# Talking-heads attention and a leaky MLP in one program: a ring of eight regrouped tiles, and a reordered end of the attention

## The chip, the cores and the metric

The kernel runs on one core of one Trainium2 chip. The metric is the device time of one execution in microseconds; lower is better. Engines are named as in the profile: PE is TensorE's matmul, PEld its weight load, DVE VectorE, ACT ScalarE, POOL GpSimd and SP SyncE, which here only issues DMAs.

## The reference, cut to what matters

Four batches, 12 heads, 448 positions, 64 channels; then an MLP on 1792 tokens of 768 channels with 2048 hidden ones. All is float32. The heads are mixed by `w_pre` ahead of the softmax and by `w_post` behind it.

```python
def _attn_ref(q, k, v, w_pre, w_post):
    scores = 1.0 / np.sqrt(q.shape[-1]) * np.matmul(q, k.transpose(0, 1, 3, 2))
    scores = np.einsum('bhij,hg->bgij', scores, w_pre)
    attn = np.exp(scores - np.max(scores, axis=-1, keepdims=True))
    attn = attn / (np.sum(attn, axis=-1, keepdims=True) + 1e-09)
    attn = np.einsum('bhij,hg->bgij', attn, w_post)
    return np.matmul(attn, v)

def reference(q, k, v, w_pre, w_post, moe_w_in, moe_w_out):
    a = _attn_ref(q, k, v, w_pre, w_post)          # B, H, S, D
    x = a.transpose(0, 2, 1, 3).reshape(B * S, H * D)
    h = x @ moe_w_in
    return np.maximum(0.01 * h, h) @ moe_w_out
```

## The kernel before, in words

**Attention.** The queries are cut into 16 chunks `n`, four to a batch, of 120, 120, 120 and 88 rows. A chunk is worked in three periods `s`, so there are 48 periods. Ten query rows with their 12 heads make a group of 120 partitions, two groups make a quad; a full chunk has six quads, the last chunk of a batch five.

- `scores(n, a)` (L184) multiplies queries and keys of a head pair into PSUM; `move` (L197) copies them on ScalarE into the score tile `s_t[n]`. This is done two chunks ahead, two pairs in a period. There are two score tiles.
- `regroup(n, a, z)` (L207) brings groups out of the score tile into `r` tiles by DMA, so that the heads of a row lie on partitions: even groups are issued by SyncE, odd ones by GpSimd. There are 12 `r` tiles (L205), used in turn. `transfers` (L610) calls it one chunk ahead, at the slots 1, 2, 4, 6, 8 and 10 of a chunk's twelve, two groups at a time (L27).
- `first(n, s, u)` (L216) mixes the heads of a quad by `w_pre` into a PSUM tile `psm` (two buffers), `maxima` (L230) takes the row maxima on VectorE, `power` (L235) the exponentials and their sums on ScalarE into `et`.
- `weights(n, s)` (L245) makes `kp` on VectorE: `w_post` times the reciprocal of the sums. `mix(n, s, part)` (L259) multiplies `et` by `kp` in two halves into `psa`; the first half is copied by ScalarE, the second by VectorE (L308). `values(n, s)` (L310) multiplies by V, one chunk behind; `keep_x` (L331) copies on VectorE and `store_x` (L338) writes to memory. `psa`, `psx` and the scores `pss` share two PSUM buffers of two banks.

Beside this the MLP's weights, which arrive as 64-bit words, are made float32 in pieces (`Narrow`, L83): a load `craw` (SyncE), two activations `z` and `w` (ScalarE, L102 and L103), three operations on VectorE, two on GpSimd, and a store (SyncE). A period spreads one piece, and two in seven of the 48; the main loop loads pieces until four less the period's count are loaded (L722).

**The order** of nearly all of the attention is written out: `pin` keeps each engine's instructions, and each queue's DMAs, in program order. So a DMA that waits holds all that stands behind it on its queue. Where `pin` is not used (the MLP's splits, sums and output), a planner orders the work by its own model of the times.

**The end of the attention** (`end_period`, L630) takes the last two chunks' six periods, without scores. It also loads the attention's output back (`load_x`, L358, four tiles to a call and two DMAs to a tile) and prepares it for the MLP (`prep_x`, L375: sums on GpSimd, a cast on ScalarE, a rest on VectorE, three or four parts in a period).

**The MLP.** Each float32 operand is split into a rounded part and a rest (`split`, L399), and each product is three matmuls. Batches `p` go in pairs; `hidden(p, j, stage)` (L472) forms two column blocks for two batches from seven products in place of eight (sums of x and w are formed ahead), in two PSUM banks `h1` and `h2`. `keep` (L454) applies the leaky maximum, `summed` (L465) adds a copied product to PSUM first. `project(u)` (L512) multiplies a hidden block by `w_out` into six PSUM banks; at a batch's end each bank is copied to an `o` tile (five of them, L803) and written out. In the pair's last units `load_x` and `prep_x` get the next pair's x (L809 to L815).

## Time and profile before

| | us |
|---|---|
| median of 3 runs | 901.79 (901.67, 901.79, 906.54) |
| profiled execution, its own time | 910.94 |
| its span, first to last instruction | 909.0 |
| PE busy | 822.5 (90%) |
| DVE busy | 590.3 (65%) |
| ACT busy | 487.4 (54%) |
| POOL busy | 170.6 (19%) |
| mean granted TensorE clock | 0.964 |

All times in rows are microseconds from the span's start unless marked ns. An engine's busy time leaves out its waits. TensorE's matmuls overlap and their ends are modelled, so a busy PE is not a PE at its peak. A granted clock of 1.00 is 2.4 GHz, of 0.50 it is 1.2 GHz; a mean between them tells the share of time at each.

### The profile page before, as it was taken

Reading aid. Unit: us, or ns where it says so; the run is one execution under the profiler, and the core shown is the slowest. Engines: PE = TensorE matmul, PEld = TensorE weight load, DVE = VectorE, ACT = ScalarE, POOL = GpSimd, SP = SyncE. Lnnn points to the kernel's source line nnn. Section 1 sums busy time; section 2 is a strip of 40 time slices with the busy share of each in tenths; the row PEclk is TensorE's granted clock in tenths of the full one; section 3 lists DMA queues with packets and bytes.
Section 4 is the critical chain, followed back from the end, with each engine's and each line's share of the span. In section 5 each row is a group of like instructions: output and inputs, shape, how many; then the busy total and the mean of one; then the engine's idle time right before and its main releaser. Section 6 shows DMA issues by size and latency. Waiting matters only on the chain.

```text
span 909.0 us, 25915 instructions
## 1 busy us (share of the span) xinstructions
PE 822.5 (90%) x10904; PEld 659.4 (73%) x10904; DVE 590.3 (65%) x1063; ACT 487.4 (54%) x952; POOL 170.6 (19%) x224
## 2 busy tenths in 40 slices
PE   7789988898889898967789999998999999999998
PEld 3356655565556555646679999997999999999897
DVE  5368666586656676766788778876756656653443
ACT  3577767687675776736254454535544333432432
POOL 4144353343443344342200000000000000000000
PEclk9699999899898999989899999999999999999999
DMA  6996969786986769473245434426634222221533
GB/s 171 266 268 197 246 214 268 194 256 211 260 241 193 235 199 271 147 203 102 82 161 172 146 122 140 148 88 197 176 104 156 80 70 74 84 70 39 161 106 112
DMA packets 90768, 150.60 MB, mean 166 GB/s; under 512 B 33001, under 2 KB 63245, under 8 KB 90653
## 3 DMA queue, kind: packets, MB, share of 16 engines
q1 hardware_dynamic: 80808, 125.50, 46.8%
q0 software_dynamic: 7296, 19.40, 8.1%
q10 hardware_dynamic: 2548, 4.06, 1.4%
q8 instruction: 86, 1.41, 0.7%
q14 instruction: 30, 0.24, 0.1%
HBM read 85.73 MB, written 23.59 MB: 120 GB/s over the span
## 4 chain that ended last, share of the span: by engine, by line
PE 72%; issue 9%; ACT 5%; DVE 5%; DMA 4%; SPq 3%; POOL 1%; POOLq 0%; DVEq 0%; ACTq 0%
PE pso L148 25%; PE psh L148 22%; PE psx L148 8%; PE pss L148 6%; PE psm L148 6%; PE psa L148 5%; ACT st L198 3%; DMA craw<-in_w_moe 2%; ACT et L241 1%; SPq L212 1%; DVE stat L231 1%; DMA qt<-in_q 1%; DMA r<-st 1%; DVE top L111 1%; SPq L370 1%
## 5 line engine op out<-in xcount | busy, mean ns | idle before, releaser
L148 PEld LDWEIGHTS psa<-kp,et 64*64 64x64 f32 x5888 | 112.4, 140 | 84.6 <-issue 52.9
L148 PE MATMUL psa<-kp,et 64*64 64x60 f32 (+1 forms) x5888 | 115.0, 222 | 39.3 <-issue 23.1
L148 PE MATMUL pso<-gh,wl 128*128 128x448 f32 x384 | 141.5, 369 | 5.1 <-DVE wl L403 3.3
L148 PE MATMUL pso<-gl,wh 128*128 128x448 f32 x384 | 140.9, 367 | 0.0
L148 PE MATMUL pso<-gh,wh 128*128 128x448 f32 x384 | 140.9, 367 | 0.0
L241 ACT ACTIVATE et<-psm,stat 128x448 f32<-128x448 f32 x184 | 116.0, 639 | 18.2 <-DVE stat L231 13.4
L198 ACT ACTIVATE st<-pss 120x896 f32<-120x896 f32 (+1 forms) x84 | 77.1, 918 | 90.3 <-PE pss L148 90.1
L231 DVE TENSOR_REDUCE stat<-psm 128x2 f32<-128x896 f32 x92 | 99.7, 1086 | 38.6 <-PE psm L148 38.5
L402 ACT CAST wh<-wo 128x768 fp32r<-128x768 f32 x64 | 53.3, 835 | 127.1 <-PE pso L148 121.5
L403 DVE TENSOR_TENSOR wl<-wo,wh 128x768 fp32r<-128x768 f32 x64 | 61.1, 956 | 86.2 <-ACT wh L402 86.2
L148 PE MATMUL pss<-kt,qt 64*56 64x448 f32 (+2 forms) x768 | 103.1, 578 | 8.5 <-DMA qt<-in_q 2.9
L148 PE MATMUL psm<-r,kpre 64*64 64x448 f32 x736 | 101.0, 595 | 8.0 <-ACT et L241 3.1
L119 POOL TENSOR_TENSOR w<-w,z 128x384 f32<-128x384 f32 x48 | 47.9, 998 | 205.1 <-ACT et L241 143.5
L148 PEld LDWEIGHTS pso<-gh,wl 128*128 128x128 f32 x384 | 72.5, 189 | 13.0 <-DVE wl L403 4.9
L148 PE MATMUL psx<-at,vt 128*64 128x120 f32 (+1 forms) x1152 | 69.9, 272 | 12.5 <-issue 4.8
L148 PEld LDWEIGHTS pso<-gh,wh 128*128 128x128 f32 x384 | 72.6, 189 | 5.8
L148 PEld LDWEIGHTS pso<-gl,wh 128*128 128x128 f32 x384 | 72.6, 189 | 5.7
L148 PEld LDWEIGHTS psx<-at,vt 128*64 128x64 f32 x1152 | 58.8, 140 | 18.4 <-ACT st L198 8.6
L333 DVE COPY xo<-psx 128x240 f32<-128x240 f32 (+1 forms) x48 | 27.4, 570 | 68.8 <-PE psx L148 68.8
L148 PEld LDWEIGHTS pss<-kt,qt 64*64 64x64 f32 (+2 forms) x768 | 29.3, 134 | 40.2 <-PE pss L148 18.1
L212 POOL DMA_DIRECT2D r<-st x90 | 53.4, 595 | 22.2 <-PE psm L148 18.9
L148 PEld LDWEIGHTS psm<-r,kpre 64*64 64x64 f32 x736 | 27.8, 141 | 39.2 <-issue 26.5
(101 smaller groups left out, 1466.0 us busy)
## 6 DMA issues: line engine op xcount, KB each, us to landing
craw<-in_w_moe SPq DMA_DIRECT2D x64, 384.0 KB
wo<-w_dram SPq DMA_DIRECT2D x64, 384.0 KB
r<-st SPq DMA_DIRECT2D x92, 210.0 KB
r<-st POOLq DMA_DIRECT2D x90, 210.0 KB, 6.4
wi<-w_dram SPq DMA_DIRECT2D x34, 384.0 KB
w_dram<-w SPq DMA_DIRECT2D x64, 192.0 KB
kt<-in_k SPq DMA_DIRECT2D x42, 112.0 KB
vt<-in_v SPq DMA_DIRECT2D x12, 384.0 KB
```

What stands on the lines that cost most here:

```text
L111: pin(nc.vector.scalar_tensor_tensor(top, z.bitcast(U32), 0x80000000, top, op0=ALU.bitwise_and, op1=ALU.bitwise_or))
L119: pin(self.joiner.tensor_mul(w, w, self.exp))
L148: pin(nc.tensor.matmul(*args, **kw))
L198: pin(nc.scalar.activation(to, ps, AF.Copy, scale=scale))
L212: pin((queues or (nc.sync, nc.gpsimd))[g % 2].dma_start(t[LOW:LOW + RH], s_t[n][g:m:m // ROWS]))
L231: pin(nc.vector.tensor_reduce(e_t[n, s][1][:, 0, 2 * u:2 * u + 2], ps[:, :, :S], axis=AX.X, op=ALU.max, negate=True))
L241: pin(nc.scalar.activation(e, ps[:, y, :S], AF.Exp, bias=st[:, 0, g:g + 1], accum_out=st[:, 1, g:g + 1]))
L333: pin(nc.vector.tensor_copy(xo_t[n][:, RUN * s:RUN * (s + 1), :m].rearrange("p a (x g) -> p a g x", x=ROWS), ps[:, :RUN, :m].rearrange("p ...
L370: pin(nc.sync.dma_start(t[:, full:], rest[:, c + HC * h]))
L402: hold(nc.scalar.copy(hi, raw))
L403: hold(nc.vector.tensor_sub(lo, raw, hi.bitcast(F32)))
```

## The change

**The ring.** Eight `r` tiles instead of twelve. `refill(count)` places the next `count` groups in order of the whole program, each by one DMA, in the tile that the group eight places earlier has left. It is called right behind the `first` calls that read those tiles: at the start 4 + 4, then 4; in the main loop behind the maxima of the period's first quad, and behind the second score pair for its second quad; in the last periods likewise. The calls from `transfers` go.

**The end.** `weights` of the next period is made at the end of this one's first mix half, instead of at the start of its own. The second quad's exponentials come behind the copy of the first mix half. `load_x` stays ahead, `prep_x` moves behind the second mix half. The very last `values` has a PSUM buffer of its own. `prep_wi(0, 2)` is pinned.

**The MLP.** `keep` is one Prelu on ScalarE. Product 7 is copied out of PSUM and product 5 is added to it there, where before product 5 was copied and product 7 stayed. The next pair's x is loaded tile by tile: eight tiles from the fourth block on, the last four in the units behind. Six `o` tiles instead of five.

```diff
@@ -24,7 +24,7 @@
 QUAD = 2 * ROWS
-REGROUP = (1, 2, 4, 6, 8, 10)
+RING = 8
@@ -201,14 +201,15 @@
-    turn = [0]
-    r_all = [p_r.tile([P, S], F32, tag=f"r{i}", name=f"r{i}") for i in range(SLOTS)]
-
-    def regroup(n, a, z, *queues):
-        m = width(n)
-        for g in range(a, min(z, m // ROWS)):
-            r_t[n, g] = t = r_all[turn[0] % SLOTS]
-            turn[0] += 1
+    r_all = [p_r.tile([P, S], F32, tag=f"r{i}", name=f"r{i}") for i in range(RING)]
+    groups = [(n, g) for n in range(NCK) for g in range(width(n) // ROWS)]
+    placed = iter(range(len(groups)))
+
+    def refill(count, *queues):
+        for _, i in zip(range(count), placed):
+            n, g = groups[i]
+            m = width(n)
+            r_t[n, g] = t = r_all[i % RING]
             pin((queues or (nc.sync, nc.gpsimd))[g % 2].dma_start(
@@ -307,12 +308,12 @@
-    def values(n, s):
+    def values(n, s, pool=ps_x):
         b, m = chunks[n][0], width(n)
...
             xo_t[n] = p_x.tile([P, NPAIR, CHUNK], F32, tag="xo", name="xo")
-        ps = ps_x.tile([P, 2, 512], F32, tag="x", name="psx")[:, 0].rearrange("p (a i) -> p a i", a=4)
+        ps = pool.tile([P, 2, 512], F32, tag="x", name="psx")[:, 0].rearrange("p (a i) -> p a i", a=4)
         w = v_t[b, s]
@@ -355,19 +356,19 @@
-    def load_x(p, c):
-        for e in range(2):
-            for h in range(2):
...
+    def load_x(p, c, tiles=range(4)):
+        for i in tiles:
+            e, h = divmod(i, 2)
...
@@ -451,15 +452,10 @@
-    def keep(p, j, m, e, c, out_of_psum=False):
+    def keep(p, j, m, e, c):
         g = pl["g"].tile([P, S], F32, tag=f"g{e}", name=f"g{e}", bufs=NF if e else 4)
         g_t[2 * p + e, 2 * j + m] = g
-        if out_of_psum:
-            t = pl["g"].tile([P, S], F32, tag="p1", name="t", bufs=1)
-            nc.scalar.activation(t, c, AF.Copy, scale=0.01)
-            nc.vector.tensor_max(g, t, c)
-        else:
-            nc.vector.scalar_tensor_tensor(g, c, 0.01, c, op0=ALU.mult, op1=ALU.max)
+        nc.scalar.activation(g, c, AF.Prelu, alpha=0.01)
@@ -486,14 +482,14 @@
             product(7, hid[2], True)
+            p7 = copy_of(hid[2], "p1")
             product(5, hid[1], False)
-            u4 = copy_of(hid[1], "p1")
-            summed(p, j, 1, 1, u4, hid[2])
+            summed(p, j, 1, 1, p7, hid[1])
         if stage == 2:
...
             product(3, hid[1], False)
-            keep(p, j, 0, 1, hid[1][:, :S], True)
+            keep(p, j, 0, 1, hid[1][:, :S])
@@ -569,12 +565,13 @@
         move_half(*scores(0, a, ((ps_x, "x"), (ps_m, "m"))[a % 2]))
-    regroup(0, 0, NJ, nc.sync, nc.scalar)
-    regroup(0, NJ, SLOTS)
+    refill(NJ, nc.sync, nc.scalar)
+    refill(RING - NJ)
     for a in range(NPAIR):
...
     dues = [first(0, 0, u) for u in range(2)]
+    refill(2 * len(dues))
     for due in dues:
@@ -600,19 +597,19 @@
-    def x_work(n, t):
+    def x_loads(n, t):
         for i in x_plan.get(t + SLOTS * (n - NCK + 2), ()):
...
                 load_x(0, -1 - i)
-            else:
+
+    def x_preps(n, t):
+        for i in x_plan.get(t + SLOTS * (n - NCK + 2), ()):
+            if i >= 0:
                 prep_x(0, *divmod(i, X_PARTS), nc.gpsimd, pin)
...
     def transfers(n, s, c):
-        b, last = chunks[n][0], n == NCK - 1
+        b = chunks[n][0]
         t = NJ * s + c
-        if not last and t in REGROUP:
-            g = 2 * REGROUP.index(t)
-            regroup(n + 1, g, g + 2)
         if t == HALF + 1 and n + 3 < NCK:
@@ -651,25 +648,36 @@
             pl.update(ws=pool("ws", 1), ps_h=pool("ps_h", 1, space=PSUM))
+            pl["ps_v"] = pools(psum, "left")("ps_v", 1, space=PSUM)
         early, late = ((2, 0), (2, 1), (2, 1), (1, 0), (0, 0), (0, 0))[at]
...
             pending = None
-        weights(n, s)
+        if at == 0:
+            weights(n, s)
         dues = [first(*left_quads.pop(0)) for _ in range(early)]
...
             maxima(*due)
+        refill(2 * early)
         for c in range(NJ):
             transfers(n, s, c)
-            x_work(n, NJ * s + c)
-        for due in dues:
+            x_loads(n, NJ * s + c)
+        for due in dues[:1]:
             power(*due)
         keep_at(mix(n, s, 0))
-        assemble()
+        for due in dues[1:]:
+            power(*due)
+        while spreading:
+            assemble()
+        if at < 5:
+            weights(*((n, s + 1) if s < 2 else (n + 1, 0)))
         keep_x(*values(n - 1, s))
         keep_at(mix(n, s, 1))
+        for c in range(NJ):
+            x_preps(n, NJ * s + c)
         for _ in range(late):
             due = first(*left_quads.pop(0))
+            refill(2)
             maxima(*due)
@@ -698,6 +706,7 @@
                 maxima(*due)
+            refill(2 * len(dues))
             transfers(n, s, 0)
@@ -716,6 +725,7 @@
                 move(*scores(to, pair + 1))
+            refill(2 * len(dues[1:]))
             if dues:
@@ -738,7 +748,7 @@
     for s in range(3):
-        keep_x(*values(NCK - 1, s))
+        keep_x(*values(NCK - 1, s, pl["ps_v"] if s == 2 else ps_x))
         for k in ((3,), (4,), (5, 6))[s]:
@@ -767,7 +777,7 @@
     load_wo(1)
-    prep_wi(0, 2)
+    prep_wi(0, 2, pin)
     load_wi(1)
@@ -795,12 +805,15 @@
                     unit += 1
+                ahead = 2 * j + stage - 6
+                if p == 0 and 0 <= ahead < 8:
+                    load_x(1, ahead // 4, (ahead % 4,))
                 narrow_late()
...
             extra.close()
-            pl["o"] = pools(mlp, "left")("o", NC - 1)
+            pl["o"] = pools(mlp, "left")("o", NC)
         while unit < (2 * p + 2) * NF - (2 if 2 * p + 2 < B else 0):
@@ -809,10 +822,10 @@
                 c, k = divmod(at, 4)
-                if k == 0:
-                    load_x(p + 1, c)
-                for k in range(2 * k, min(2 * k + 2, X_PARTS)):
-                    prep_x(p + 1, c, k)
+                for i in range(2 * k, min(2 * k + 2, X_PARTS)):
+                    prep_x(p + 1, c, i)
+                if c == 1:
+                    load_x(p + 1, 2, (k,))
```

## Rows read from the trace of the kernel before

**Rows 1.** Windows: length, busy PE, PEld, DVE, ACT, POOL (count), clock, DMA share, GB/s.

```profile
40.00:382.50 342.50, 300.25 (x7359) 201.57 (x7351) 229.17 (x462) 247.61 (x531) 137.35 (x172) 0.96 0.81 230
382.50:440.60 58.10, 40.74 (x1047) 30.93 (x1047) 40.56 (x73) 28.40 (x68) 21.54 (x21) 0.91 0.45 125
397.00:412.00 15.00, 9.13 (x197) 5.75 (x189) 9.19 (x13) 7.24 (x20) 5.95 (x6) 0.77 0.72 214
440.60:467.80 27.20, 19.73 (x140) 17.15 (x139) 21.01 (x37) 12.77 (x23) 0.56 (x1) 0.86 0.49 158
444.00:454.00 10.00, 6.81 (x41) 6.05 (x40) 6.91 (x14) 3.02 (x6) 0.00 (x0) 0.66 0.47 132
467.80:607.40 139.60, 139.60 (x676) 128.08 (x677) 112.10 (x206) 64.79 (x109) 0.00 (x0) 0.99 0.44 137
```

**Rows 2.** Timeline of the start: start, length, engine, line, count, [idle before <-releaser].

```profile
13.69 10.18 SPq L212 DMA_DIRECT2D r<-st  x6
...
30.84 2.17 PE L148 MATMUL pss<-kt,qt 64*64 64x448 f32 x5 [2.92 <-DMA qt<-in_q]
```

**Rows 3.** Timeline of period n = 8, s = 0: SyncE, TensorE, then ScalarE.

```profile
228.02 0.81 SPq L212 DMA_DIRECT2D r<-st  x1
228.88 3.18 SPq L96 DMA_DIRECT2D craw<-in_w_moe  x3
...
228.88 0.93 PE L148 MATMUL psm<-r,kpre 64*64 64x448 f32 x8
...
235.12 0.56 ACT L102 ACTIVATE z<-craw 128x384 f32<-128x384 f32 x1 [0.77 <-DMA craw<-in_w_moe]
...
236.69 0.92 ACT L198 ACTIVATE st<-pss 120x896 f32<-120x896 f32 x1 [0.56 <-PE pss L148]
```

**Rows 4.** Waits (total, times, longest); DMA issues (us to landing); chain of waits.

```profile
ACT z L102 <- DMA craw<-in_w_moe: 8.0, 6, 2.5
PE psa L148 <- DVE kp L253: 7.7, 5, 2.6
PE psa L148 <- ACT at L308: 7.6, 4, 4.7
...
r<-st POOLq DMA_DIRECT2D x90, 210.0 KB, 6.4
...
286.60 7.60 DMA craw<-in_w_moe
```

**Rows 5.** Timeline of the end, second of the last six periods.

```profile
398.51 1.44 POOL L382 TENSOR_TENSOR xr<-xr 128x448 f32<-128x448 f32 x1 [8.66 <-DMA xr<-x_dram]
399.98 0.56 ACT L394 CAST xh<-xr 128x448 fp32r<-128x448 f32 x1 [6.12 <-POOL xr L382]
403.93 1.93 PE L148 MATMUL psa<-kp,et 64*64 64x60 f32 x64 [4.71 <-ACT at L308]
```

**Rows 6.** Timeline from the last values to the second MLP unit.

```profile
446.89 0.50 DVE L333 COPY xo<-psx 128x200 f32<-128x200 f32 x1
447.44 2.27 PE L148 MATMUL psx<-at,vt 128*64 128x100 f32 x24 [3.19 <-DVE xo L333]
...
460.91 0.47 PE L148 MATMUL psh<-xh,wdl 128*128 128x448 f32 x1 [1.33 <-DVE c L466]
...
462.69 0.55 ACT L102 ACTIVATE z<-craw 128x384 f32<-128x384 f32 x1 [2.48 <-DMA craw<-in_w_moe]
...
467.78 0.74 PE L148 MATMUL psh<-xh,wal 128*128 128x448 f32 x1 [2.94 <-DVE g L460]
```

**Rows 7.** Groups of instructions: count, busy us, mean ns, idle before.

```profile
L459 ACT ACTIVATE t<-psh 128x448 f32<-128x448 f32 x16 | 8.7, 543 | 17.1 <-PE psh L148 17.1
L529 ACT ACT_TABLE_LOAD x1 | 1.3, 1283 | 0.8 <-PEq L845 0.8
```

**Rows 8.** Timeline of the MLP: two single stalls.

```profile
633.04 0.47 PE L148 MATMUL pso<-gh,wl 128*128 128x448 f32 x1 [3.31 <-DVE wl L403]
...
848.65 0.62 DVE L523 COPY o<-pso 128x448 f32<-128x448 f32 x1 [4.12 <-DMA out_t<-o]
```

More of the change, by code (lines that the diff above doesn't have):

```diff
@@ L356 @@
     free = lambda ins: ins
-    def load_x(p, c):
-        for e in range(2):
-            for h in range(2):
-                t = pl["xr"].tile([P, S], F32, tag="xr", name="xr")
-                xr_t[p, c, h, e] = t
-                full = S // CHUNK * CHUNK
-                src = x_dram[2 * p + e]
-                pin(nc.sync.dma_start(
-                    t[:, :full].rearrange("p (n i) -> p n i", i=CHUNK),
-                    src[:, :NC * full].rearrange("p (n c i) -> p n c i", c=NC, i=CHUNK)[:, :, c + HC * h],
-                ))
-                rest = src[:, NC * full:].rearrange("p (c i) -> p c i", c=NC)
-                pin(nc.sync.dma_start(t[:, full:], rest[:, c + HC * h]))
+    def load_x(p, c, tiles=range(4)):
+        for i in tiles:
+            e, h = divmod(i, 2)
+            t = pl["xr"].tile([P, S], F32, tag="xr", name="xr")
+            xr_t[p, c, h, e] = t
+            full = S // CHUNK * CHUNK
+            src = x_dram[2 * p + e]
+            pin(nc.sync.dma_start(
+                t[:, :full].rearrange("p (n i) -> p n i", i=CHUNK),
+                src[:, :NC * full].rearrange("p (n c i) -> p n c i", c=NC, i=CHUNK)[:, :, c + HC * h],
+            ))
+            rest = src[:, NC * full:].rearrange("p (c i) -> p c i", c=NC)
+            pin(nc.sync.dma_start(t[:, full:], rest[:, c + HC * h]))
     X_PARTS = 7
```

## The prediction, made before the result was known

> **What bounds the kernel now.** I read the windows by stage first, then the waits by engine, then single stretches of the timeline. The profiled execution took 910.94 us, of which the span is 909.0; the median of the runs is 901.79, so this execution is 9.15 us above it. I make the sum against the profiled execution and shift it by that difference.
>
> In the attention stage (40 to 382.5 us) TensorE is busy in 300.25 of 342.5 us at a granted clock of 0.96, and the DMA engines have a share of 0.81 [rows 1]. The reader is to see a stage without one full engine: a period of work (two quads, two score pairs, one mix, one set of values) is a chain through TensorE, ScalarE and VectorE, and what is lost is lost where a link is late. From 382.5 to 440.6 (the last periods, without scores) TensorE works 40.74 of 58.1 us, and from 440.6 to 467.8 (attention's last values and the first MLP unit) 19.73 of 27.2. In the MLP (467.8 to 607.4) TensorE is full: 139.60 of 139.60 [rows 1]. Work moved between VectorE and ScalarE is worth nothing there unless a PE wait ends on it. So the change can gain at the two ends and at single stalls, and its ring acts on the 342 us of attention.
>
> **The change part by part.**
>
> *Ring of eight, at the start.* Before, SyncE issues six regroup DMAs in a row, 10.18 us or 1.70 each, and behind them the load of the third chunk's queries, for which TensorE waits 2.92 us [rows 2]. With eight tiles instead of twelve, four of the six stand ahead of that load; the other two come behind it. 2 x 1.70 = 3.4 us earlier covers the wait. Bounds 0 and -2.9; I take -2, since the remaining DMAs still share the engines. Four memsets on VectorE fall away under the first loads: nothing.
>
> *Ring of eight, in the periods.* A tile is now refilled right behind the `first` that reads it, so each refill waits for TensorE in its own period; with twelve tiles it waited only for the chunk's scores. What is queued behind the second refill on SyncE are the craw loads. In most periods these have two periods of lead, and the delay costs nothing. But after each of the six periods that spread two pieces (n odd, s = 2), nothing is left loaded, and the first craw of the next period is spread in that same period. There, before: regroup at 228.02 (0.81 us to issue), craw at 228.88, the second `first` from 228.88 for 0.93, the spread at 235.12 after a wait of 0.77, and the next score copy at 236.69 [rows 3]. After: the refill issues at 229.81, the craw at 229.81 + 0.81 = 230.62 or later, 1.8 us later. ScalarE has 0.56 us of idle left ahead of that copy, so the copy comes 1.8 - 0.56, about 1.3 us, late. Six times 1.3 is +8; I take +7. ScalarE waits for craws 8.0 us in 6 places in all before [rows 4], so the path is already tight. Bounds: 0 (the DMA engines were the limit and the later craw lands in less), and +14 (1.8 each and a clock drop or two).
>
> *The same refill and the score tile.* The last regroup of a chunk must land before the score copy two chunks on overwrites its source. Issued at 229.81 (by the period in rows 3) and landing after a median of 6.4 us [rows 4], it is there at 236.2, against the copy at 236.69: 0.5 us to spare. The slowest landing on the chain of waits is 7.60 [rows 4]: 0.7 us late. Ten of the chunks are in this case (of full width but the first), so bounds 0 and 10 x 0.7 = +7; I take +2, since the median fits.
>
> *Weights a unit ahead.* TensorE waits for `kp` 7.7 us in 5 places [rows 4], all behind VectorE's copies of the mix before. Now kp is made before those copies. Next late is then the PSUM buffer that the first mix half holds until ScalarE's copy. Bounds 0 and -7.7; I take -5.
>
> *Copies among exponentials, preparations of x last.* TensorE waits 7.6 us for the `at` copy in 4 places [rows 4]; 4.71 of it at 403.93. There ScalarE stood 6.12 us at a cast, behind GpSimd, which stood 8.66 for an x tile, and the exponentials and the copy were queued behind the cast [rows 5]. The clock over these 15 us was 0.77, which is another 3.5 us [rows 1]. Now the casts come behind the copy and the second mix half. But the tiles land no sooner (two refills are issued ahead of their loads on SyncE), and behind the casts stand the exponentials of the late quad, for which the next period's second `first` waits. So a part of this stall moves rather than goes. Bounds 0 and -11; I take -4.
>
> *More PSUM for values.* The last values wait 3.19 us for the xo copy of the first, which VectorE makes only at 446.89 [rows 6], and the clock over 444 to 454 falls to 0.66, 3.4 us more [rows 1]. A third buffer takes the wait away, and pinning `prep_wi(0, 2)` takes VectorE's early work from before that copy. Bounds 0 and -6.6; I take -5. The price: the next weight tile is freed, and loaded, later.
>
> *Seventh product kept, keep by Prelu.* In the first unit, which has no projection to cover it, TensorE waits 1.33 us for VectorE's sum and 2.94 us for the kept g [rows 6]. Product 7 is copied out under product 5's nine matmuls, so the first wait goes; the second shrinks to one activation, about 0.54 us by the slope copy that it replaces [rows 7]. But ScalarE stands 2.48 us for a craw there [rows 6], and Prelu can be queued behind that. Bounds 0 and -4.3; I take -3. Everywhere else TensorE is full and the move from VectorE to ScalarE is free. The trace of before shows one table load, 1.28 us [rows 7]; if Prelu's table is another one, a second such load stands once ahead of the first Prelu: bounds 0 and +1.3, taken as 0, under the unit's products.
>
> By the Trainium skill (ScalarE: Activation LUTs, "What ACT_TABLE_LOAD costs") a switch of sets is about 2.66 us with its drain. With that figure in the sum, the forecast would be 2.7 us higher; no run here shows the drain.
>
> *x tiles one by one, a sixth output tile.* The stall of 3.31 us at 633.04 stands behind VectorE, held by preparations of freshly loaded x tiles [rows 8]; two thirds of the tiles are now loaded units earlier. Bounds 0 and -5 (with a clock drop); I take -3. VectorE waits 4.12 us for an output DMA at 848.65 [rows 8], but TensorE has the next unit's first five column blocks to do meanwhile, and only what lies beyond them counts: bounds 0 and -4.1, I take -1.5, nearer nothing.
>
> Sum: -2 + 7 + 2 - 5 - 4 - 5 - 3 - 3 - 1.5 = -14.5. Against 910.94 that is 896.4; against the median **887**.
>
> **The rivals.** *The ring is free.* If craws and regroups land early enough, +9 falls away: -23.5, and with some of the bounds more, 868 to 878. For it: the wait before the spread is 0.77 us only, and 0.56 us of idle follows on ScalarE [rows 3]. Against: nothing in that period is left loaded.
>
> *The stalls of the end move.* The casts' wait for x tiles goes into the next period's exponentials (the -4 becomes 0), kp's wait becomes one for the PSUM buffer (-5 becomes -2), VectorE's pinned preparation delays the first unit (-8 becomes -4). Then -14.5 + 4 + 3 + 4 = -3.5: 898. For it: VectorE is busy in 21.01 of 27.2 us there [rows 1].
>
> *The ring makes it slower.* If the second refill holds SyncE so long that the spread waits in ordinary periods too, each pays the 1.3 us. It decides from 23.5 / 1.3 = 18 of the 42 periods on; with 30 of them, 39 - 23.5 = +15.5, or 917. For it: the DMA share of 0.81 [rows 1]. Against: the lead of two periods.
>
> *It doesn't do what it says.* Much of the MLP's order is not pinned and is the planner's, so kept product and Prelu may sit elsewhere than written. That is inside the second rival.
>
> **How the numbers follow.** Forecast 0.5 (its own range 877 to 896), ring free 0.2, stalls moved 0.2, slower 0.1. The range 868 to 903 takes in the first three and leaves out most of the last and a tail. About 1% is what a measurement of this kernel can tell from no change, that is 892.8 to 910.8. Faster: five sixths of 0.5, all of 0.2 and a little of the third, 0.65. Slower 0.08, same 0.27.
>
> **What would show it.** At the start, TensorE's wait for the queries under 1 us. In the periods n even, s = 0: craw 1.8 us later against the second `first`, a wait of 2 us or more at its spread. From 382 to 441 some 9 us less, with no wait for kp. No gap ahead of the last values, none over 1 us after the first unit, none at the second x preparation. The forecast is wrong if attention between 40 and 382 changes by more than 15 us, if a new wait for regroups stands ahead of score copies, or if the last six periods keep their length.

## The result, and the profile after

The changed kernel takes 894.11 us (median of 18 runs, 884.95 to 901.41), the kernel before beside it 906.9 us (18 runs). The ratio is 0.9847, 95% interval 0.9819 to 0.9874: 13.9 us less, between 11.4 and 16.4. (Ratios here leave out executions that lie over 1.5% above their kernel's fastest, so they are not the quotients of the medians.) The prediction had 14.5 less, the range held the time, and the time itself lies 7 us above the 887 named, of which 5 are the median that it was shifted to (901.79 of three runs, now 906.9). The two profiled executions differ by 20.6 us (spans 909.0 and 888.4), more than the runs do: the one before lies 4.0 us above its kernel's median, the one after 3.9 below. The MLP's repeated units take the same time to 0.1 us in both; the attention does not repeat so well. Six of the kernels below share the changed kernel's code up to the values of period 41, and in these seven traces they begin anywhere from 365.7 to 376.7 us. A difference of a few us between single traces there tells nothing.

By stages of the trace the kernel after lies thus; it answers to [rows 1], with the same columns (length, then busy PE, PEld, DVE, ACT, POOL with counts, clock, DMA share, GB/s):

```profile
40.00:372.90 332.90, 291.86 (x7318) 196.38 (x7310) 226.47 (x456) 243.81 (x526) 140.25 (x174) 0.97 0.83 235
372.90:431.70 58.80, 40.85 (x1047) 31.82 (x1047) 38.90 (x70) 27.70 (x66) 17.60 (x18) 0.85 0.48 133
385.70:404.60 18.90, 8.18 (x188) 5.57 (x180) 9.84 (x17) 7.49 (x20) 5.37 (x5) 0.70 0.74 206
431.70:437.20 5.50, 5.50 (x86) 4.93 (x86) 4.01 (x4) 0.56 (x1) 4.71 (x4) 1.00 0.01 3
437.20:455.20 18.00, 11.79 (x55) 9.58 (x54) 13.48 (x25) 11.43 (x22) 0.00 (x0) 0.99 0.61 190
587.40:656.80 69.40, 69.40 (x344) 64.38 (x344) 46.44 (x73) 34.90 (x60) 0.00 (x0) 1.00 0.48 140
```

The windows are cut at the same work as before. To be seen: the attention up to the values of period 41 is 9.6 us shorter; the last six periods are as long as they were (58.1 and 58.8); the three last values have lost their gap (10.2 us before, 5.5 now, no half clock); the first unit of the MLP is 1.1 us longer; and the stretch with the second x preparation is full (75.3 us before, 69.4 now). Two views say why the last six periods did not get shorter. The first is TensorE's waits there (total, times, longest):

```profile
PE psm L148 <- DMA r<-st: 9.8, 1, 9.8
PE psa L148 <- ACT at L309: 3.6, 2, 2.7
PE psa L148 <- ACT at L307: 2.1, 1, 2.1
PE psa L148 <- DVE kp L254: 1.3, 1, 1.3
```

Before, the 7.7 us for kp and 7.6 us for `at` of [rows 4], with 0.9 for the same copy in a period of one quad (L306) and 1.2 for an exponential, come to 17.4 us; after, these four rows come to 16.8, and 17.9 with three of under 0.7 us. The waits that the change was to take away did go (kp 7.7 to 1.3, the copy 8.5 to 5.7), and one new wait of 9.8 us for a regrouped tile took their place. The second view is the timeline of that wait, SyncE's queue first, then POOL, VectorE and TensorE; it answers to [rows 5]:

```profile
391.83 0.48 SPq L371 DMA_DIRECT2D xr<-x_dram  x1
392.42 0.85 SPq L123 DMA_DIRECT2D w_dram<-w  x2
395.43 0.92 SPq L410 DMA_DIRECT2D wi<-w_dram  x2
396.44 3.12 SPq L213 DMA_DIRECT2D r<-st  x3
...
392.67 1.44 POOL L383 TENSOR_TENSOR xr<-xr 128x448 f32<-128x448 f32 x1 [7.01 <-DMA xr<-x_dram]
394.05 0.59 POOL L213 DMA_DIRECT2D r<-st  x1
...
394.74 1.56 DVE L396 TENSOR_TENSOR xl<-xr,xh 128x448 fp32r<-128x448 f32 x1 [1.61 <-ACT xh L395]
396.22 2.08 DVE L232 TENSOR_REDUCE stat<-psm 128x2 f32<-128x896 f32 x2
...
389.69 1.72 PE L148 MATMUL psm<-r,kpre 64*64 64x448 f32 x16
401.21 1.77 PE L148 MATMUL psm<-r,kpre 64*64 64x448 f32 x8 [9.81 <-DMA r<-st]
```

Three queues that work in order hold the next product. SyncE comes to the refill at 396.44, behind sixteen x loads (until 392.3), two stores and the MLP's first weights, which themselves waited from 393.3 to 395.4. POOL comes to its half at 394.05, behind a preparation that stood 7.01 us for an x tile. VectorE takes the maxima of a product that ended at 391.4 only at 396.22, behind the split of the same preparation.

In the attention two things changed against each other. TensorE's waits there, before (40 to 382 us) and then after (40 to 373); "issue" is time in which it waited for nothing that the profile shows:

```profile
PE psa L148 <- issue: 23.1, 16, 3.3
PE psx L148 <- issue: 8.3, 3, 4.8
```

```profile
PE psa L148 <- issue: 13.8, 13, 4.7
PE psa L148 <- ACT st L198: 10.5, 8, 2.4
PE psx L148 <- issue: 4.2, 2, 2.4
```

The 10.5 us are the ring's price, with 1.5 more that the profile puts to VectorE (at 236.66 us): TensorE waits for a score copy that comes late. Of these 12.0 us, 6.9 stand in five places behind a wait of ScalarE for a held weight piece, as predicted. The other 5.1 stand in four places where the late copy is the first of a chunk, which overwrites a score tile; at one of them, chunk 7, the profile names the regroup that the copy waits for (ScalarE, then TensorE):

```profile
148.06 0.92 ACT L198 ACTIVATE st<-pss 100x896 f32<-100x896 f32 x1 [3.67 <-DMA r<-st]
149.03 1.16 PE L148 MATMUL psa<-kp,et 64*64 64x60 f32 x64 [1.54 <-ACT st L198]
```

One of the periods with a held weight piece, chunk 8, s = 0, answers to [rows 3] (timeline, SyncE, then ScalarE):

```profile
226.51 0.81 SPq L213 DMA_DIRECT2D r<-st  x1
227.37 3.49 SPq L96 DMA_DIRECT2D craw<-in_w_moe  x3
...
234.83 0.55 ACT L102 ACTIVATE z<-craw 128x384 f32<-128x384 f32 x1 [3.81 <-DMA craw<-in_w_moe]
```

ScalarE's waits in the whole kernel answer to [rows 4]:

```profile
ACT z L102 <- DMA craw<-in_w_moe: 20.1, 8, 4.1
ACT st L198 <- DMA r<-st: 3.7, 1, 3.7
```

The second `first` ended at 226.48, the craw was issued 0.9 us behind it (before: with its start), and its wait went from 0.77 to 3.81 us. And yet the attention is not longer: the "issue" gaps (all of 0.25 us or more) fell from 33.3 us to 17.9 beside it. What that time is, the experiments were to find.

At the end of the attention TensorE no longer waits ahead of the last values, but stands 3.42 us at the second MLP unit. The profile names VectorE there; by the program the product needs the PSUM bank that the unit's last Prelu frees, and that ends at 455.11. On ScalarE this Prelu stands behind a cast that waits for a weight tile, and behind the two activations of a weight piece. The tile is now freed and loaded later: its load is issued 8.6 us behind the last values, where it was issued 7.7 us ahead of their end (443.17). The timeline of TensorE, then ScalarE, answers to [rows 6]:

```profile
435.28 1.25 PE L148 MATMUL psx<-at,vt 128*64 128x100 f32 x24
455.16 0.74 PE L148 MATMUL psh<-xh,wal 128*128 128x448 f32 x1 [3.42 <-DVE top L108]
...
452.30 0.51 ACT L403 CAST wdh<-wi 128x384 fp32r<-128x384 f32 x1 [0.86 <-DMA wi<-w_dram]
454.59 0.52 ACT L458 ACTIVATE g<-psh 128x448 f32<-128x448 f32 x1
```

### The profile page after: what moved, and what is told of

It reads as the page before. It is cut to its first block, busy times and chain, and to the rows that moved or that the text cites. A ratio compares the mean times of both kernels' runs of the same rounds, so it can differ in the third digit from the quotient of the medians.

```text
span 888.4 us, 25847 instructions
## 1 busy us (share of the span) xinstructions
PE 810.4 (91%) x10904; PEld 652.0 (73%) x10904; DVE 554.3 (62%) x995; ACT 510.5 (57%) x1000; POOL 173.0 (19%) x224
## 3 DMA queue, kind: packets, MB, share of 16 engines
q8 instruction: 86, 1.41, 0.7%
## 4 chain that ended last, share of the span: by engine, by line
PE 69%; issue 8%; DMA 7%; ACT 6%; DVE 5%; SPq 2%; POOL 1%; ACTq 0%; POOLq 0%; DVEq 0%
PE pso L148 26%; PE psh L148 22%; PE psx L148 7%; PE psa L148 5%; PE psm L148 4%; PE pss L148 4%; ACT st L198 3%; DMA craw<-in_w_moe 3%; ACT et L242 2%; DMA r<-st 1%; DVE stat L232 1%; DMA xr<-x_dram 1%; DVE top L111 1%; PE idle L148 1%; SPq L213 1%
## 5 line engine op out<-in xcount | busy, mean ns | idle before, releaser
L148 PEld LDWEIGHTS psa<-kp,et 64*64 64x64 f32 x5888 | 109.4, 140 | 84.0 <-issue 36.8
L148 PE MATMUL psm<-r,kpre 64*64 64x448 f32 x736 | 91.5, 564 | 13.5 <-DMA r<-st 10.8
L148 PE MATMUL pss<-kt,qt 64*64 64x448 f32 (+2 forms) x768 | 94.8, 556 | 4.9 <-DVE st L202 2.6
L148 PE MATMUL psx<-at,vt 128*64 128x120 f32 (+1 forms) x1152 | 73.1, 279 | 11.6 <-issue 4.2
L334 DVE COPY xo<-psx 128x240 f32<-128x240 f32 (+1 forms) x48 | 27.3, 568 | 82.5 <-PE psx L148 82.5
L148 PEld LDWEIGHTS psx<-at,vt 128*64 128x64 f32 x1152 | 61.6, 145 | 18.0 <-ACT st L198 9.7
L148 PEld LDWEIGHTS psm<-r,kpre 64*64 64x64 f32 x736 | 25.4, 137 | 40.7 <-issue 28.3
L309 ACT COPY at<-psa 128x960 f32<-128x960 f32 x44 | 43.1, 980 | 14.0 <-PE psa L148 13.9
```

Of the source, the lines that this page charges most:

```text
L148: pin(nc.tensor.matmul(*args, **kw))
L309: pin(copy(to, src))
L334: pin(nc.vector.tensor_copy(xo_t[n][:, RUN * s:RUN * (s + 1), :m].rearrange("p a (x g) -> p a g x", x=ROWS), ps[:, :RUN, :m].rearrange("p ...
```

## Experiments

My theory after the traces: (1) the ring delays the weight pieces, as predicted, but pays for it by thinning the late "issue" gaps; (2) in the last periods one wait replaced another, and several queues hold it. The rival to (1): the ring does nothing, the spread of runs does; to (2): one queue alone holds it. Ratios are to the kernel before, run beside each.

**The ring undone, and the ring alone.** The first is the changed kernel with twelve tiles, the second the kernel before with eight:

```diff
-    refill(2 * len(dues))          # behind each first
+    if not last and t in REGROUP:  # set out over the period before
+        regroup(n + 1, g, g + 2)
```

> The changed kernel with the ring alone undone: twelve regrouped tiles and the loads set out over the period before, as in the kernel before; the new end is kept. By the prediction's sum the ring costs 7 us in the periods (weight pieces held on SyncE) and 2 us at the refill against the score copy, and gives 2 us at the start: this kernel should be about 7 us faster than the changed kernel, near 0.977 of the kernel before, with the z waits for craw back at 8 us in all and the second period's wait for the query back at 2.9 us. Rival: the periods absorb the later weight pieces, because the spreads that wait are not what ends a period; then it loses only the start's 2 us (0.987 of before), or up to 9 us if the periods gained from the ring as the two profiles seem to show (values of period 41 start 9.6 us sooner after the change): 0.995.

> The kernel before with the ring alone: eight tiles, refilled behind each first; nothing of the new end. By the prediction's sum it is slower than the kernel before by 7 + 2 - 2 = 7 us (1.008). Rival one, the periods absorb the held weight pieces: -2 us from the start (0.998). Rival two, the ring speeds the periods: up to -9.6 us in the attention, of which the end may give back what the second half of the refill costs behind the x loads (0.990 to 1.0).

Measured: 0.9839 (0.9771 to 0.9907) without the ring, against 0.9847 with it; 1.003 (0.9992 to 1.0067) with the ring alone, +2.7 us. The +7 that I predicted lies at or outside the edge of both; the ring is worth nothing that these runs can measure. ScalarE's waits for craw went where they should in the periods: 7.0 us in 5 places with twelve tiles, 20.0 in 6 with eight. TensorE's in the attention with twelve tiles, then with eight alone:

```profile
PE psa L148 <- issue: 20.8, 12, 3.7
```

```profile
PE psa L148 <- issue: 14.3, 11, 3.9
PE psa L148 <- ACT st L198: 12.0, 8, 2.5
```

The same exchange in another pair, and the same split: 7.0 of the 12.0 us stand behind held pieces and 5.1 behind a chunk's first copy. The "issue" gaps come to 33 and 30 us in the two traces with twelve tiles and all loads (the values of period 41 at 382.5 and 381.9 us) and to 13 to 21 us in the eleven with eight; the two sets do not overlap. The traces favour the ring by 8 us and more up to there, where the runs show nothing. Much of that may be the choice of execution: both traces with twelve tiles are of executions some 4 us above their kernels' medians (910.94 on 906.9, 895.40 on 891.67), and those of the two kernels beside them lie 2 to 4 below. That something pays for the 12 us the runs show as well; that it is the thinner gaps rests on the traces, and why a ring thins them stays open. In the last six periods the ring is not the cause of the length: with twelve tiles and the new end they take 57.3 us, and TensorE waits 6.8 us for r in two places.

**Weight pieces ahead of the second refill.** One block of SyncE's program is moved up:

```diff
+            while len(loaded) < 4 - count and pieces:
+                loaded.append(Narrow(p_c, *pieces.pop(0)))
             refill(2 * len(dues[1:]))
```

> The changed kernel with the loads of the weight pieces set on SyncE ahead of the second refill of each period, not behind it. Theory of the prediction (the waits of the weight pieces lengthen the periods): the z waits for craw fall from 20.1 us to about 6 and the time by 7 us, to 0.977 of the kernel before. Rival: ScalarE has slack in those periods, the waits go and the time stays (0.983 to 0.986), as the attention did not get longer though the waits came. Against both: the refill now stands behind 384 KB loads and the next period's scores come later, so that the time rises (0.987 to 0.99).

Measured: 0.9915 (0.9875 to 0.9954), slower than the changed kernel: the third outcome. ScalarE's waits in the attention:

```profile
ACT st L198 <- DMA r<-st: 13.5, 3, 9.6
ACT z L102 <- DMA craw<-in_w_moe: 9.4, 5, 3.0
```

The pieces come sooner (19.5 to 9.4 us), and now score copies wait for a refill that has not yet read their source (3.7 to 13.5, one of 9.6). The two share one queue; whichever is second is paid for. This is the step that the prediction priced at +2, shown by its reverse.

**The second x loads later.** `x_plan` only: the second batch of x loads goes from step 0 to step 4.

```diff
-    x_plan = {0: [-1, -2], 4: [0, 1, 2], ...
+    x_plan = {0: [-1], 4: [-2, 0, 1, 2], ...
```

> The changed kernel with the second batch of eight x tile transfers issued one third of a period later, so that period 43's refill stands on SyncE ahead of it; nothing else moves. Theory: the 9.8 us in which TensorE waits for the regrouped tiles at 394 us, and the half clock around it (13.7 us at 1.2 GHz), come from the second half of the refill standing behind sixteen x transfers on SyncE's queue. Then the wait goes, and the stretch from the values of period 41 to those of the last chunk falls from 58.8 to about 48 us, the time to 0.973 to 0.975 of the kernel before. Rival one: the x tiles are then late for the preparations, and the wait moves to them or to the spreads: 0 to -5 us (0.980 to 0.985). Rival two: the regrouped tiles wait for the move of the scores or for TensorE itself and not for SyncE: no change in the wait (0.985).

Measured: 0.9845 (0.9789 to 0.9901), the stretch 57.8 us. The refill on SyncE still came at 396.8, now behind the MLP's first weights, which waited 4.1 us ahead of it, and TensorE's wait kept its length under another name:

```profile
PE psm L148 <- ACT et L242: 8.3, 1, 8.3
```

So the theory of one queue is not enough: SyncE was still held, and what ended the wait was an exponential, behind maxima that VectorE takes at 399.17, behind a split. From this I formed the theory of waits side by side.

**The preparations behind the late quad, then all three queues freed.** The first kernel swaps two blocks of `end_period`, `x_preps` and the loop over `late`. The second also has the later x loads, and `load_wi(0)` behind the refill:

```diff
-            load_wi(0)
             store_x(n - 2)
...
         refill(2 * early)
+        if at == 3:
+            load_wi(0, pin)
```

> The changed kernel with the preparations of the x tiles set behind the late quad of each of the last periods (its product, refill, maxima and exponentials), not ahead of it; nothing else moves. Theory: at 389 to 405 us two waits stand side by side, the half of the refill behind the x loads and the wait for w_dram on SyncE, and VectorE's maxima of the late quad behind the split of a preparation that waits for an x tile (maxima at 396.2 where the product ended at 390.7). This kernel takes away the second alone: PE still waits some 9 us for r, and the stretch from the values of period 41 to those of the last chunk stays within 2 us of 58.8, the time at 0.984 to 0.987 of before. Rival: the order on VectorE and POOL alone sets the wait (POOL's half of the refill also stands behind a preparation): then the 9.8 us fall to under 3 and the stretch to about 51 us (0.976).

> As the kernel with the preparations behind the late quad, and besides the second batch of x loads a third of a period later and the first load of the MLP's weights behind the refill of its period, so that neither SyncE nor VectorE nor POOL holds the regrouped tiles. Theory of two waits side by side: only now does the 9.8 us wait go, and the half clock (13.7 us) with it; the stretch from the values of period 41 to those of the last chunk falls from 58.8 to 46 to 50 us and the time to 0.970 to 0.977 of before. Rival: the x tiles, now later, hold the casts and the second unit of the hidden sums, which gives back what was gained (0.982 to 0.987); the stretch falls and the one from the last values to the second unit grows from 18 to 25 us or more.

Measured: 0.9867 (0.9816 to 0.9918) and a stretch of 60.2 us for the first, with the wait for r at 10.3 us: as the theory has it. 0.9769 (0.9706 to 0.9831) and 56.3 us for the second, by the ratio 7 us less than the changed kernel, with intervals that just overlap. There the wait for r is gone, and TensorE's waits in the stretch are

```profile
PE psa L148 <- ACT at L309: 7.4, 3, 4.5
PE psm L148 <- ACT et L242: 3.1, 1, 3.1
```

Freeing VectorE and POOL gave nothing, and with SyncE freed too the wait for r is gone, as the theory has it; SyncE alone, free of both its loads, was not run, so that it takes all three is argued. The size was wrong: 2.5 us gained in the stretch, not 9 to 13. The period with the long wait fell from 18.9 to 12.1 us, and two later ones wait for the copy of `at` again (2.07 and 4.46 us): ScalarE makes it behind three casts and behind exponentials that wait for VectorE, which stands at the splits of the same preparations. That is the rival's give-back, though in the periods and not at the second unit (16.9 us). In the trace 7.2 of the 10.6 us gained lie before the values of period 41, which this edit does not touch.

**Fewer weight loads in the attention.** The kernel before, whose first four weight pieces are used again:

```diff
+            if bufs[0] == 4 and len(raws) >= 4:
+                self.raw = raws[len(raws) % 4]
+                ...
+                return
```

> The kernel before with the first four weight pieces loaded and then used again in all the periods: 45 loads of 384 KB less (17 MB of some 75 MB that the attention moves), everything else in place; the weights of the second half are then not the reference's. It asks what the gaps before the mix and the values are (33.6 us of TensorE between 40 and 382 us that no semaphore explains). Theory: TensorE runs out of instructions there, because a 16 KB piece of its program (86 such transfers on a queue of their own) lands late behind the data on the DMA engines; with less data the gaps fall to under 20 us, and the values of period 41 begin 8 us sooner or more (below 374 us; time 0.985 to 0.992). Rival: the gaps do not hang on the traffic (order of semaphores, or a fixed cost at certain places of the program): they stay at 28 us or more and the time falls only by the z waits' share, 0 to 3 us.

Measured: 0.9708 (0.9644 to 0.9772), and period 41's values begin at 347.2 us where they began at 382.5. TensorE's waits up to 360 us:

```profile
PE psx L156 <- issue: 6.3, 4, 3.2
PE psa L156 <- issue: 5.4, 9, 1.1
```

33.3 us of gaps became 11.5, and half clock in the attention 27.3 us became 3.4. A gap can be seen in the kernel before at 168 us, first in TensorE's timeline:

```profile
167.83 0.51 PE L148 MATMUL psa<-kp,et 64*64 64x60 f32 x20
171.64 1.38 PE L148 MATMUL psa<-kp,et 64*64 64x60 f32 x43 [3.30 <-issue]
```

Then among the DMA queues from 168.0 to 171.6 us (packets, MB, share of the engines):

```profile
q8 instruction: 1, 0.02, 1.8%
```

And by windows over the gap and over the half clock that began in it:

```profile
168.30:171.60 3.30, 0.04 (x2) 0.00 (x0) 0.87 (x1) 0.27 (x1) 0.65 (x2) 0.80 0.85 240
170.30:177.10 6.80, 5.46 (x68) 3.32 (x71) 2.57 (x6) 1.53 (x3) 0.00 (x0) 0.50 0.66 201
```

Queue q8 carries 86 transfers of 16 KB in the whole kernel, 1.41 MB, one for every 256 of TensorE's 22,038 instructions in the trace. The one here began at 168.99 and ended at 170.04, with TensorE still, and TensorE started 1.6 us later. Of the gaps of over 0.8 us that no semaphore explains, between 40 us and period 41's values, 14 of 14 in the kernel before, 6 of 6 in the changed one, 5 of 5 here, and 113 of 113 over the 14 traces end 1.2 to 1.7 us behind the end of a q8 transfer. So TensorE stood for a piece of its own program. What is late is the piece's start: in the 14 gaps of before it began between 1.5 us ahead of TensorE's stop and 2.0 behind it, and took 0.9 to 1.4 us, with fewer loads no less (0.9 to 1.3 in 5). That the gaps shrink with 17 MB of loads less (DMA share 0.81 to 0.67) is what this run shows; which queue or engine holds the pieces, and whether traffic alone does it, it does not.

**Three edits of the MLP undone.** The leaky step on VectorE and product 7 not kept; x tiles by fours; five o tiles.

```diff
-            p7 = copy_of(hid[2], "p1")
             product(5, hid[1], False)
-            summed(p, j, 1, 1, p7, hid[1])
+            u4 = copy_of(hid[1], "p1")
+            summed(p, j, 1, 1, u4, hid[2])
...
-                if c == 1:
-                    load_x(p + 1, 2, (k,))
+                if k == 0:
+                    load_x(p + 1, c)
```

> The changed kernel with three edits of the MLP undone together, each in its own stretch of the trace: product 7 not kept and the leaky step on VectorE (all hidden units), the x tiles of the second pair of batches loaded four at a time when the first preparation is due (before the second pair's first product), five o tiles for six (last projections). By the prediction's sum 3 + 3 + 1.5 = 7.5 us come back. By the trace of the changed kernel: the hidden units of the first pair 0.5 to 2 us, the stretch from the last unit of the first pair to the first product of the second pair 69.3 to 75.3 us, the last stretch 86.1 to 88.2: about 9 us, 0.994 of before. Rival: the second table of ScalarE (the leaky step) costs what the moved work saves, so that the first of the three is 0 or less and the sum is 7 to 8 us.

Measured: 0.9988 (0.9941 to 1.0034), some 13 us slower than the changed kernel. By windows (first unit, second unit, second x preparation, last projections):

```profile
439.50:458.80 19.30, 12.06 (x56) 9.56 (x54) 16.34 (x30) 11.47 (x21) 0.00 (x0) 0.97 0.56 177
458.80:482.50 23.70, 23.18 (x100) 20.83 (x101) 20.64 (x40) 9.97 (x19) 0.00 (x0) 0.88 0.52 159
593.10:669.40 76.30, 72.99 (x344) 66.09 (x343) 51.57 (x82) 36.67 (x62) 0.00 (x0) 0.96 0.51 146
810.30:899.20 88.90, 87.75 (x424) 79.07 (x422) 35.16 (x49) 29.60 (x47) 0.00 (x0) 1.00 0.32 98
```

Against the changed kernel's 18.0, 21.7, 69.4 and 86.1 these are +1.3, +2.0, +6.9 and +2.8, 13 us as in the runs and not the 9 forecast. The second unit's +2.0 goes with a lower clock (0.88 for 0.93) and isn't shown to be the edits': the unit takes 21.6 to 21.8 us in the three other kernels without them, and 20.2 to 21.9 in the ten with them. In two other kernels with these edits in place (preparations behind the late quad, weights in their own period) the last two stretches take 70.5 and 87.3 us, so the x tiles are worth 6 to 7 us and the o tile 1.7 to 2.8. The units between, which have projections, stay at 121.6 us: nothing gained there, as predicted.

**Weights in their own period again.**

```diff
-        if at == 0:
-            weights(n, s)
+        weights(n, s)
...
-        if at < 5:
-            weights(*((n, s + 1) if s < 2 else (n + 1, 0)))
```

> The changed kernel with the weights of the mix computed in their own period again in the last five periods (in the kernel before the mix waited 7.7 us for them in five places). By the prediction's sum their place a unit ahead is worth 5 us: the stretch from the values of period 41 to those of the last chunk would grow from 58.8 to about 64 us, the time to 0.990 of before. Rival: the waits for kp come back, some 1.3 us at each of five places, but the waits for r and for the copy behind them shrink by as much, since the next product stands still for a tile that comes when it comes: 58 to 60 us and no change in the time (0.983 to 0.987).

Measured: 0.9902 (0.986 to 0.9943), 5 us more than the changed kernel, and a stretch of 72.3 us where some 64 were forecast:

```profile
PE psa L148 <- DVE kp L254: 16.8, 5, 6.9
PE psm L148 <- DMA r<-st: 8.5, 1, 8.5
```

The wait for r did not give way, so the rival falls in the trace; by the ratio (its interval just overlaps the changed kernel's) the forecast of 5 us holds. The waits are longer than the 7.7 us of before: at 425.7 us VectorE makes kp behind the copies of the mix and three splits of preparations. In the new order the weights have to be early.

**The last values in two buffers.**

```diff
-        keep_x(*values(NCK - 1, s, pl["ps_v"] if s == 2 else ps_x))
+        keep_x(*values(NCK - 1, s))
```

> The changed kernel with the last values in the two buffers of before again. By the prediction's sum (5 us) and by the two traces (10.23 to 5.47 us): the three values of the last chunk take 10 us from the first to the end, the third stands 3 us behind a split of the MLP's weights on VectorE, and the later stages begin 4.8 us later. Rival: the gap was the half clock's doing and not the buffer's: 6 to 7 us.

Measured, in a single execution (889.47 us): the values take 11.55 us, with the wait of before:

```profile
437.57 2.27 PE L148 MATMUL psx<-at,vt 128*64 128x100 f32 x24 [4.51 <-DVE xo L334]
```

But the first unit behind them takes 13.3 us for 18.0: the loads that hold ScalarE at its end, the weight tile and behind it on SyncE a weight piece, are issued only 2.0 us later, counted from the first of these values (16.1 and 17.2 us behind it for 14.1 and 15.3), where the values end 6.1 us later. Both together are 24.9 us against 23.5: of the 5 or 6 us at the gap some 1.4 remain.

**Fewer pieces in the attention, and this with the freed queues.** 40 pieces in the attention, one in each period, and 24 in the MLP:

```diff
-    late_pieces = [... if f >= NF // 2 and j > 1]
+    late_pieces = [... if f >= NF // 4 and j > 1]
-            count = (at + 1) * 48 // 41 - at * 48 // 41 if at < 41 else 0
+            count = 1 if at < 40 else 0
-                if stage and 5 <= j <= 6:
+                if j < 5:
                     narrow_late()
```

> The changed kernel with 40 weight pieces narrowed in the attention for 48, one in each period, and 24 in the MLP for 16, two for one in most steps there. It moves 3 MB of loads and the double periods out of the attention. Theory (the attention's excess over 7.2 us for each period hangs on the traffic: 45 loads less gave 35 us, 0.8 us each): 8 loads less give 6 us, the z waits for craw go from 20 us to under 6, and the MLP, bound by TensorE, hides the eight pieces: 0.976 to 0.980 of before. Rival: VectorE, in order, takes the pieces ahead of the splits that the MLP's products wait for, and the ten or so units of the first pair grow by 0.5 to 1.5 us each: 0.985 to 1.0.

> The 40 pieces together with the end in which SyncE, VectorE and POOL do not hold the regrouped tiles (the preparations behind the late quad, the second batch of x loads later, the first weights of the MLP behind the refill). If the two gains add up: 0.9769 less 0.006, some 0.971 of before (880 us). Rival: the MLP gives the pieces' gain back: 0.975 to 0.985.

Measured: 0.9646 (0.9593 to 0.9699), 873.81 us, and 0.9618 (0.9543 to 0.9692), 874.22 us. Both beat the changed kernel and their own forecasts; the two can't be told apart, so what the freed queues add to the 40 pieces is not shown. In the first, period 41's values begin at 356.8 us, ScalarE's wait for craw falls to 9.0 us, and TensorE's wait for score copies in the attention shows what went:

```profile
PE psa L148 <- ACT st L198: 1.8, 3, 0.8
```

The gaps are as in the changed kernel (19.1 us); the 10.5 us behind late score copies are down to 1.8. The MLP hides the eight pieces (121.7 for 121.6 us, 69.9 for 69.4). Of the 16.0 us that the attention is shorter in these two traces, 8.7 are those waits and some 3.5, by estimate, the clock (10.2 us at half for 17.1); the rest stays open. My 6 us from the traffic alone was too little, as the double periods went with it.

## Why the prediction was right or wrong

The sum came out by luck, because two misses cancelled: +9 for the ring that was not there, and -9 at the last periods that did not come. By the prediction's own signs it was wrong in two places: the last six periods kept their length, and a new wait of 3.7 us for a regroup stands ahead of a score copy.

Where the gain lies shows best in the kernel before and the changed one with twelve tiles, whose traces reach the values of period 41 at 382.5 and 381.9 us. Of the 15.3 us between their spans, 0.8 lie in the last six periods, 4.4 at the last values, 1.6 in the first two MLP units, 6.0 at the second x preparation and 2.1 in the last projections. The forecast had 9, 5, 3, 3 and 1.5: most of the gain is the MLP's, and the largest part of it is the x tiles.

- *Start, -2:* right. Period 3's first product begins at 48.22 for 50.23, and no wait for the queries over 0.5 us is left.
- *Ring in the periods, +7:* the mechanism was right, in place and size: the same six places, waits of 2.2 to 4.1 us for 0.1 to 1.9, and TensorE pays 6.9 us behind them. The step failed in that it took this for the ring's whole effect. The 31 us of "issue" in those periods are in no term; they are late program pieces, and the trace with the ring has 15 us fewer of them and 10 us less half clock. Its net by the runs is +2.7 us, with an interval from -0.7 to +6.1; the two traces show 7.6 us less, about what their executions lie off their medians. The first rival (the ring is free) named the outcome, but its reason, that the pieces land early enough, is refuted.
- *Refill and score copy, +2:* mis-sized. TensorE pays 5.1 us behind the first score copies of chunks 3, 4, 7 and 12, in four places and not in ten; at chunk 7 the copy waits 3.67 us for the regroup. The 7.60 us that the prediction took for the slowest regroup is the landing of a weight piece in [rows 4].
- *Weights ahead, -5, and copies among exponentials, -4:* the waits went as said (-6.4 and -2.8), the stage kept its length. The failed step is the sentence that only "a part of this stall moves": all of it did. I had seen that the x tiles land no sooner and that the late quad stands behind the casts, but priced neither the other half of the refill behind x loads and weights on SyncE nor the half clock that a 9.8 us stop brings (clock 0.70 over 18.9 us). My second rival, at 898, came nearest: it had the stall moving, but to the exponentials and the PSUM buffer, not to the regrouped tiles.
- *More PSUM, -5:* -4.8 at the gap, but 1.1 back at the next unit and, by the experiment (one execution), some 1.4 net. The price that I named, the later weight tile, is what took it, with the weight piece behind it: ScalarE's last Prelu of the unit stands behind both, and TensorE 3.42 us at 455.16.
- *Product 7 and Prelu, -3:* the first unit gains 1.3 us by the experiment, and 2.4 to 3.6 with the two PSUM buffers of before (13.3 us with the edits, 15.8 to 17.0 in three kernels without, which differ at the end of the attention too); in the pair of traces that same stand hides it. The wait for the kept g did not shrink to the 0.54 us that I took: Prelu is queued behind a weight piece, as I had feared, and TensorE stands 1.2 to 3.4 us there in ten kernels, against 2.0 to 4.0 in four without it. The table load is the one of before, 1.28 us: there was no second.

```profile
L525 ACT ACT_TABLE_LOAD x1 | 1.3, 1283 | 0.8 <-PEq L858 0.8
```

- *x tiles, -3, and the o tile, -1.5:* right in place; the first mis-sized, 6 to 7 us: the stall of 3.31 us was the largest there, not all of it; the second 1.7 to 2.8.

## What to carry to other kernels

When a wait is taken away, list every in-order queue that the next product hangs on, and ask which of them is free sooner: here SyncE, POOL and VectorE held the same product, and the two kernels that freed part of them gained nothing that the runs could tell. "Issue" time of an engine with tens of thousands of small instructions is worth a look at the queue that brings its program: it fell from 33.3 to 11.5 us with 17 MB of loads less, though not with 3 MB less, and in the kernel before it took more time than all of TensorE's semaphore waits of the stage. Two kinds of loads on one queue price each other; the way out was to move fewer of them through the crowded stage, since the MLP took eight pieces for nothing.

## What the runs showed of the hardware

- TensorE can run out of program. Its 16 KB pieces take about 1 us each and it starts again 1.2 to 1.7 us behind their end, so that the gap is the longer the later the piece begins; five of the six longest such gaps of the kernel before have 3.4 or 6.8 us at a granted clock of 0.50 beginning in them or just behind them. With 45 loads of 384 KB less, gaps and half clock went from 33.3 and 27.3 us to 11.5 and 3.4. By the Trainium skill (Runtime: NRT & Kernel Launch, "Instruction fetch mechanics") the program is streamed in 16 KiB blocks on a queue of the sequencer's own and the cost of a block's edge is mostly hidden; the trace agrees with the size and the queue, and not with the cost, which was 33 us of 342.
- The time of the kernel before spreads from 900.3 to 920.0 us over 18 runs, and the same attention code took 11 us more or less from trace to trace. The late pieces fall in the attention; that they are the cause of the spread was not tested.
